# Roots of a row norm laid into memory word by word and read back in token order (attention, dense layer and routed experts on one core)

## The chip, the cores and the metric

One core of a Trainium2 chip runs the whole program. The metric is the device time of one execution in microseconds (us). Of the kernel before, three runs are given: 649.17, 650.56 and 652.78 us, median 650.56.

The engines: TensorE (PE; PEld is its weight load), VectorE (DVE), ScalarE (ACT), GpSimd (POOL) and SyncE (SP), which here only issues transfers. ScalarE issues a few transfers too; a `q` behind an engine's name (ACTq, SPq) marks what its sequencer does. Each engine works through its own list of instructions in order and waits for the others by semaphores.

## The reference

Attention with a bucket mask, then a dense gated layer with a norm of its rows, then a layer of eight routed experts:

```python
scores = scale * np.matmul(q, k.transpose(0, 1, 3, 2))
scores = np.where(mask, scores, -1000000000.0)
...
x = np.ascontiguousarray(attn_out.transpose(0, 2, 1, 3)).reshape(B * S, H * D)   # 1536 tokens x 512
rms = np.sqrt(np.mean(x * x, axis=-1, keepdims=True) + 1e-06)
xn = x / rms * rms_g
g = xn @ w_gate
silu = g * (1.0 / (1.0 + np.exp(-g)))
val = xn @ w_val
x = (silu * val @ w_out)                                                          # then the experts
```

The change touches only how `1 / rms` comes to where `x / rms * rms_g` is formed.

## The kernel before

**Stages.** The attention works through 96 units (a head's 128 queries against 768 keys): a score product on TensorE (`qk`, L530 and L532), the row maximum on VectorE (`stats`, L545), the exponential on ScalarE (`expo`, L559), a scaling by the row sum on GpSimd (`scales`, L554), transposes on TensorE (`back`, L568) with copies out of PSUM by ScalarE or VectorE (`emptied`, L572), and the product with v (L589). The order of all of this is written out by hand: the table `PLAN` gives each step a due time in thousandths of a unit, `attention` collects the steps with `at` and issues them sorted by it. Steps of the dense layer that prepare its weights (L238 to L252) and the norm of its first block of tokens are sorted in among them.

The dense layer (`moe1`) takes three blocks of 512 tokens, and in each twelve slices of 128 of the 1536 hidden features, 36 steps in all. A step splits a slice's weights into a high and a low part (`split`, L317 on ScalarE, L318 on VectorE or GpSimd), forms the gate and value products on TensorE (L345 to L347), the activation (L749 to L753), the low half of the hidden values on VectorE (`h_low`, L758), and adds the down product of the step before (L769 to L771; L771 is the matmul that reads what L758 writes). Products are made of three matmuls of high and low parts each. The weights of later slices are converted on the way (`cv` and `rebias`, L244 to L252 on VectorE, L791 on ScalarE).

**The norm** (`xnorm`, one for each block b): x stands as features by tokens, four chunks of 128 features by 512 tokens. `square` and `add` form the sums of squares; `mean` sums them over the partitions by TensorE, so that one row holds the 512 means; `turn` (L287) moves them by four transfers into a tile `r` of 128 partitions by 4 words, so that token t * 128 + p stands at partition p, word t; `root` (L291, L292 on GpSimd) takes the power -0.5 there; `lay` (L295, issued by ScalarE) writes the 512 roots to a line of device memory, the last row of the output, which is overwritten at the end; `spread` (L298, issued by ScalarE for block 0, by SP for the others) reads that line back into all 128 partitions as `rb`; `scale` (L301 on VectorE, one for each of four chunks) forms x * rms_g * root; `high` (L304, ScalarE) and `low` (L307, VectorE for block 0, GpSimd for the others) split the result for the matmuls.

`lay` writes the line so that each partition's four words stand together, 128 runs of 16 bytes: word 4 * p + t of the line is the root of token t * 128 + p. `scale` therefore reads `rb` with a step of four words, through the views that `ch_` and `rearrange("p (q t) -> p t q")` make.

**Order around the change.** Block 0's norm runs in the attention, at the due times of `PLAN["xn"]` (its entries in order: `square`, `add`, `mean`, `turn`, `root`, `lay`, `spread`, `scale`, `high`, `low`). The norms of blocks 1 and 2 run in the dense block before: with o the first step of that norm, `mean` and `turn` are in step o + 5, `root` in o + 6, `lay` in o + 7 in the list `cal` (after the step's gate and value part), `spread` in o + 7 in the list `post` (after the step's down product), the four `scale` with their `high` in o + 8 and o + 9, the `low` one step after each. SP's and ScalarE's lists hold other transfers and work, and what stands behind a waiting entry waits too.

Of the kernel before, what the change touches and what calls it, by code (L numbers as in the profile page):

```python
# [13 lines left out]
ALU = mybir.AluOpType  # L14
AX = mybir.AxisListType
P = 128
# [29 lines left out]
    "cv": (-4, 4300, 7612, 8983, 10967),  # L46
    "late": 2000,
    "v": 11280,
    "xn": ((54501, 56400), (57300, 58235, 59400), 60900, 62000, 64000, 65000, 69000, (74588, 92089, 73653, 83058), (86240, 93654, 83020, 84060), (89992, 93958, 86081, 95569)),
    "splits": ((-6894, 1, 0, 0), (-10825, 1, 0, 1), (-4899, 0, 0), (1381, 1, 1, 0), (8244, 1, 1, 1)),  # L50
    "ahead": ((215, 2), (3057, 4), (4742, 6), (17871, 8)),
    "batches": (2, 2, 3, 2, 3, 2, 3, 2, 3, 2),
# [27 lines left out]
def tile_kernel(  # L80
# [17 lines left out]
    nc = tc.nc  # L98
# [12 lines left out]
    TPB = TB // P  # L111
# [7 lines left out]
    STT = nc.vector.scalar_tensor_tensor  # L119
# [12 lines left out]
    def f32(ap):  # L132
        return ap.bitcast(F32)
# [19 lines left out]
    def ch4(ap):  # L153
        return ap.rearrange("p (k n) -> p k n", k=4)

    xyt = [ch4(XY[:, i * 2048 : (i + 1) * 2048]) for i in range(3)]
# [34 lines left out]
    gcol = cp.tile([P, NK], F32, name="gcol")  # L191
# [64 lines left out]
    def xpart(b, lo, k):  # L256
        o = X_AT[b] + lo * 2048 + k * TB
        return rg(o, TB)

    def xnorm(b):  # L260

        xf = ch4(BB[:, 0:2048])
        rb = EX[:, 1536:2048]
        sq = rb[:, 0:P]
        line = out[NT - 1 : NT, :]
        st = {}

        def ch_(ap):
            return ap.rearrange("p (t q) -> p t q", t=TPB)

        def square(hf):
            sl = slice(2 * hf, 2 * hf + 2)
            nc.scalar.activation(out=xf[:, sl], in_=xyt[b][:, sl], func=AF.Square)

        def add(x):
            i, j = ((0, 2), (1, 3), (0, 1))[x]
            TT(out=xf[:, i], in0=xf[:, i], in1=xf[:, j], op=ALU.add)

        def mean(ps):
            for t in range(TPB):  # L280
                mm(ps[32 * t : 32 * t + 32, 0:P], lhsT=ones[:, 0:32], rhs=xf[:, 0, t * P : (t + 1) * P], start=True, stop=True)
            (copyV if b else copyA)(out=sq, in_=ps[:, 0:P])

        def turn():
            r = st["r"] = sp.tile([P, 2 * TPB], F32, tag="r", name="r", bufs=2)
            for t in range(TPB):
                dma(out=r[:, t : t + 1], in_=sq[32 * t : 32 * t + 1, :])  # L287

        def root():
            r = st["r"]  # L290
            PTS(r[:, 0:TPB], r[:, 0:TPB], 1.0 / DM, 1e-6, ALU.mult, ALU.add)  # L291
            PTT(out=r[:, TPB:], in0=r[:, 0:TPB], in1=half, op=ALU.pow)  # L292

        def lay():
            nc.scalar.dma_start(out=line.rearrange("o (p t) -> p (o t)", p=P), in_=st["r"][:, TPB:])  # L295

        def spread():
            (dma if b else nc.scalar.dma_start)(out=rb, in_=line.broadcast_to([P, TB]))  # L298

        def scale(k):  # L300
            STT(out=ch_(xf[:, k]), in0=ch_(xyt[b][:, k]), scalar=gcol[:, k : k + 1], in1=rb.rearrange("p (q t) -> p t q", t=TPB), op0=ALU.mult, op1=ALU.mult)  # L301

        def high(k):
            copyA(out=xpart(b, 0, k), in_=xf[:, k])  # L304

        def low(k):
            (PTT if b else TT)(out=xpart(b, 1, k), in0=xf[:, k], in1=f32(xpart(b, 0, k)), op=ALU.subtract)  # L307

        return dict(square=square, add=add, mean=mean, turn=turn, root=root, lay=lay, spread=spread, scale=scale, high=high, low=low)


# [39 lines left out]
    cal = []  # L351
# [327 lines left out]
    def attention():  # L679
# [33 lines left out]
        for x in range(12, 15):  # L713
            at(1000 * (NU - 9) + 500, cv_load, x)
        xn = xnorm(0)
        sq, ad, me, tu, ro, ly, sd, sc, hi_, lo_ = PLAN["xn"]
        for x in range(2):
# [20 lines left out]
    def moe1(rt):  # L738
        total = NBLK * NF
        hs, acc = {}, {}  # L740
        cal = defaultdict(list)
        win = defaultdict(list)
        post = defaultdict(list)
# [52 lines left out]
        for b in range(1, NBLK):  # L796
            xn = xnorm(b)
            o = (b - 1) * NF + (0 if b == 1 else 1)
            for x in range(2):
                cal[o + x].append(lambda f=xn["square"], x=x: f(x))  # L800
            for x in range(3):
                cal[o + 2 + x].append(lambda f=xn["add"], x=x: f(x))
            win[o + 5].append(xn["mean"])
            cal[o + 5].append(xn["turn"])
            cal[o + 6].append(xn["root"])
            cal[o + 7].append(xn["lay"])
            post[o + 7].append(xn["spread"])
            for k in range(NK):
                cal[o + 8 + k // 2].append(lambda xn=xn, k=k: (xn["scale"](k), xn["high"](k)))
                cal[o + 9 + k // 2].append(lambda f=xn["low"], k=k: f(k))  # L810
# [540 lines left out]
    with tc.manual_schedule():  # L1351
        rt = routing()
        attention()
        moe1(rt)
        moe2(rt)
# [92 lines left out]
```

## Time and profile before

| what | value |
|---|---|
| median of three runs | 650.56 us (649.17 to 652.78) |
| the profiled execution's own time | 648.81 us |
| its span, first to last instruction | 646.9 us |
| TensorE busy | 633.8 us, 98% |
| VectorE busy | 533.7 us, 83% |
| ScalarE busy | 399.9 us, 62% |
| GpSimd busy | 268.2 us, 41% |
| granted TensorE clock | 0.998 of full |
| queue of ScalarE's transfers | 720 packets, 0.37 MB |

How to read it: the busy shares are means over stages with different limits. The profiled execution is one execution; its time is its span and some 2 us around it. In a table of waits, each row says which engine waited for which, how long in total, how many times, and the longest. In a timeline each row is one instruction or a run of equal ones: start, busy time, engine, line of the kernel, operation, output and inputs, and in brackets the engine's idle time just before it and what ended it.

### The profile page before, as it was taken

What the parts mean: (1) busy time and instruction counts of PE and PEld (TensorE: products, weight loads), DVE (VectorE), ACT (ScalarE), POOL (GpSimd) and SP (SyncE); (2) the same over time, 40 slices, a digit from 0 to 9 for tenths busy, and PEclk for the clock granted to TensorE, in tenths of its full rate; (3) what the DMA queues carried; (4) which work ended last, traced back from release to release, by engine and by line L of the source; (5) the groups of instructions that cost most, each with busy time, mean ns of one, the idle gap of its engine ahead of it and who ended that gap; (6) DMA issues with size and microseconds to landing.
All of it is one profiled execution on the core that took longest, in us unless ns stands there. A gap on an engine that the chain in (4) does not pass through costs nothing. (4 is left out here: it accounts for less than half of the span.)

```text
span 646.9 us, 10512 instructions
## 1 busy us (share of the span) xinstructions
PE 633.8 (98%) x3598; PEld 504.0 (78%) x3599; DVE 533.7 (83%) x906; ACT 399.9 (62%) x724; POOL 268.2 (41%) x299
## 2 busy tenths in 40 slices
PE   8999999999999999999899999999999999999996
PEld 6777777777777778888788888888888888888884
DVE  6888888898978839998966787899999476999994
ACT  6787888988789746555444333344334353888782
POOL 4677576676756703551622212341124325111211
PEclk9999999999999999999999999999999999999999
DMA  8726538356252215552301000003304015999930
GB/s 250 189 65 193 148 103 218 104 166 151 83 125 103 66 33 183 180 166 74 140 20 53 1 2 0 17 1 128 137 24 173 0 71 175 387 390 389 389 130 26
DMA packets 45991, 84.96 MB, mean 131 GB/s; under 512 B 5708, under 2 KB 19228, under 8 KB 45808
## 3 DMA queue, kind: packets, MB, share of 16 engines
q1 hardware_dynamic: 43856, 80.70, 38.8%
q0 software_dynamic: 1360, 3.20, 1.4%
q8 instruction: 29, 0.48, 0.3%
q10 hardware_dynamic: 720, 0.37, 0.2%
q14 instruction: 26, 0.21, 0.1%
HBM read 67.95 MB, written 5.25 MB: 113 GB/s over the span
## 5 line engine op out<-in xcount | busy, mean ns | idle before, releaser
L318 POOL TENSOR_TENSOR RG<-WW,RG 128x512 fp32r<-128x512 f32 x35 | 68.7, 1962 | 190.1 <-ACT RG L317 182.4
L345 PE MATMUL PS<-RG 128*128 128x512 f32 x288 | 112.5, 391 | 0.0
L346 PE MATMUL PS<-RG 128*128 128x512 f32 x288 | 112.1, 389 | 0.0
L347 PE MATMUL PS<-RG 128*128 128x512 f32 x288 | 112.1, 389 | 0.0
L545 DVE TENSOR_REDUCE peak<-PS 128x1 f32<-128x768 f32 x96 | 91.5, 953 | 20.7 <-PE PS L532 16.0
L559 ACT ACTIVATE WW<-PS,shape 128x768 f32<-128x768 f32 x96 | 95.5, 1000 | 10.9 <-DVE shape L546 9.7
L753 ACT CAST RG<-BB 128x512 fp32r<-128x512 f32 x36 | 22.4, 622 | 109.9 <-DVE BB L751 109.9
L554 POOL TENSOR_SCALAR WW<-WW,rsum 128x768 f32<-128x768 f32 x96 | 87.8, 926 | 4.8
L568 PE MATMUL PS<-cst,WW 128*128 128x128 f32 x576 | 81.4, 277 | 1.0 <-POOL WW L554 0.8
L568 PEld LDWEIGHTS PS<-cst,WW 128*128 128x128 f32 x576 | 64.1, 140 | 20.9 <-POOL WW L554 9.5
L1121 DVE TENSOR_TENSOR RG<-WW,RG 128x1024 fp32r<-128x1024 f32 x64 | 75.2, 1218 | 4.5 <-ACT RG L1119 2.4
L318 DVE TENSOR_TENSOR RG<-WW,RG 128x512 fp32r<-128x512 f32 x73 | 61.4, 879 | 8.3 <-ACT RG L317 8.3
L317 ACT CAST RG<-WW 128x512 fp32r<-128x512 f32 x108 | 61.4, 618 | 7.7 <-PE PS L771 5.0
L1119 ACT CAST RG<-WW 128x1024 fp32r<-128x1024 f32 x64 | 63.9, 1053 | 1.1 <-PE PS L1176 0.8
L345 PEld LDWEIGHTS PS<-RG 128*128 128x128 f32 x288 | 54.1, 188 | 11.8 <-issue 0.8
L347 PEld LDWEIGHTS PS<-RG 128*128 128x128 f32 x288 | 54.1, 188 | 11.3
L346 PEld LDWEIGHTS PS<-RG 128*128 128x128 f32 x288 | 54.1, 188 | 11.1
L771 PE MATMUL PS<-RG 128*128 128x512 f32 x144 | 56.3, 391 | 1.7 <-DVE RG L758 1.7
L769 PE MATMUL PS<-RG 128*128 128x512 f32 x144 | 56.4, 392 | 0.0
L770 PE MATMUL PS<-RG 128*128 128x512 f32 x144 | 56.1, 389 | 0.0
L530 PE MATMUL PS<-RG 128*128 128x512 f32 x192 | 55.5, 369 | 0.2 <-ACT WW L559 0.2
L909 DVE CUSTOM_DVE_ANT_0 EX<-XY,SS 128x512 f32<-128x512 f32 x64 | 50.1, 782 | 1.6
(202 smaller groups left out, 1238.8 us busy)
## 6 DMA issues: line engine op xcount, KB each, us to landing
WW<-in_w SPq DMA_DIRECT2D x32, 1024.0 KB
RG<-RG SPq DMA_DIRECT2D x28, 384.0 KB
WW<-in_kq SPq DMA_DIRECT2D x7, 768.0 KB
SS<-in_wo SPq DMA_DIRECT2D x9, 512.0 KB
SS<-in_wg SPq DMA_DIRECT2D x8, 512.0 KB
SS<-in_wv SPq DMA_DIRECT2D x8, 512.0 KB
WW<-in_v SPq DMA_DIRECT2D x8, 384.0 KB
XY<-in_wg SPq DMA_DIRECT2D x4, 512.0 KB
```

The costliest lines, as they stand in the source:

```text
L317: copyA(out=hi, in_=src)
L318: sub(out=lo, in0=src, in1=f32(hi), op=ALU.subtract)
L345: mm(o, lhsT=h[:, k], rhs=xpart(b, 0, k), start=(k == 0), stop=False)
L346: mm(o, lhsT=h[:, k], rhs=xpart(b, 1, k), start=False, stop=False)
L347: mm(o, lhsT=l[:, k], rhs=xpart(b, 0, k), start=False, stop=(k == NK - 1))
L545: red(out=a[:, 1:2], in_=u_st[u][:, 0:S], axis=AX.X, op=ALU.max, negate=True)
L554: PTS(e_t(x), e_t(x), rsum[:, x % NS : x % NS + 1], 1.0, ALU.mult, ALU.mult)
L559: nc.scalar.activation(out=e_t(u), in_=s[:, 0:S], func=AF.Exp, bias=c, scale=b, accum_out=sums[:, u % NS : u % NS + 1])
L568: nc.tensor.transpose(ps[:, x * P : (x + 1) * P], e_t(u)[:, kt * P : (kt + 1) * P], ident)
L769: mm(acc[t], lhsT=hh[:, sl], rhs=oh, start=(f == 0), stop=False)
L1119: copyA(out=hi[:, sl], in_=src[:, sl])
L1121: f(out=lo[:, sl], in0=src[:, sl], in1=f32(hi[:, sl]), op=ALU.subtract)
```

## The change

Three edits. The line of roots is written so that word t * 128 + p is the root of token t * 128 + p: every one of the 512 words goes to a place of its own (step of 128 words in the line for the words of a partition). `scale` reads `rb`, and x, and writes its output, without the reordering views; the helper `ch_` goes. And the places in the order: in the dense blocks `lay` moves from step o + 7 to the end of step o + 6 (list `post`), and in the attention, in the table, `root` is due at 63700 (64000 before), `lay` at 64500 (65000) and `spread` at 71000 (69000).

```diff
-... 60900, 62000, 64000, 65000, 69000, ...
+... 60900, 62000, 63700, 64500, 71000, ...
...
-        def ch_(ap):
-            return ap.rearrange("p (t q) -> p t q", t=TPB)
-
...
         def lay():
-            nc.scalar.dma_start(out=line.rearrange("o (p t) -> p (o t)", p=P), in_=st["r"][:, TPB:])
+            nc.scalar.dma_start(out=line.rearrange("o (t p) -> p (o t)", p=P), in_=st["r"][:, TPB:])
...
         def scale(k):
-            STT(out=ch_(xf[:, k]), in0=ch_(xyt[b][:, k]), scalar=gcol[:, k : k + 1], in1=rb.rearrange("p (q t) -> p t q", t=TPB), op0=ALU.mult, op1=ALU.mult)
+            STT(out=xf[:, k], in0=xyt[b][:, k], scalar=gcol[:, k : k + 1], in1=rb, op0=ALU.mult, op1=ALU.mult)
...
-            cal[o + 7].append(xn["lay"])
+            post[o + 6].append(xn["lay"])
```

The lists of TensorE, VectorE, GpSimd and SP keep their order; only ScalarE's changes, in three places. (Behind the removed helper the changed file is three lines shorter, so L295 is L292 there, L298 is L295, L317 is L314, L572 is L569 and so on.)

ScalarE in the dense layer, the step in which block 1's norm lays its line (L791 is a weight conversion, L317 the weights' high parts, L749 and L753 the activation). Before:

```order
L791 ACTIVATE BB<-WW 128x512
L791 ACTIVATE SS<-SS 128x512
L317 CAST RG<-WW 128x512 x3
L749 ACTIVATE BB<-PS 128x512
L753 CAST RG<-BB 128x512
L295 DMA out<-r 128x4
```

Of the change:

```order
L788 ACTIVATE BB<-WW 128x512
L788 ACTIVATE SS<-SS 128x512
L292 DMA out<-r 128x4x1
L314 CAST RG<-WW 128x512 x3
L746 ACTIVATE BB<-PS 128x512
L750 CAST RG<-BB 128x512
```

The write has moved ahead of the step's three casts and its activation; in block 2 it moves in the same way.

ScalarE in the attention, where block 0's line is laid and read (L572 copies transposes out of PSUM, L559 is the exponential, L599 the copy of the product with v). Before:

```order
L599 COPY XY<-PS 128x256
L572 COPY BB<-PS 128x3x128
L295 DMA out<-r 128x4
L572 COPY BB<-PS 128x3x128
L559 ACTIVATE WW,sums<-PS,shape 128x768 x2
L572 COPY EX<-PS 128x3x128 x2
L572 COPY BB<-PS 128x3x128 x2
L559 ACTIVATE WW,sums<-PS,shape 128x768 x2
L572 COPY WW<-PS 128x3x128
L599 COPY XY<-PS 128x256
L572 COPY WW<-PS 128x3x128
L298 DMA EX<-out 128x512
```

Of the change:

```order
L292 DMA out<-r 128x4x1
L569 COPY BB<-PS 128x3x128 x2
L556 ACTIVATE WW,sums<-PS,shape 128x768 x2
L569 COPY EX<-PS 128x3x128 x2
L569 COPY BB<-PS 128x3x128 x2
L556 ACTIVATE WW,sums<-PS,shape 128x768 x2
L569 COPY WW<-PS 128x3x128
L596 COPY XY<-PS 128x256
L569 COPY WW<-PS 128x3x128 x2
L556 ACTIVATE WW,sums<-PS,shape 128x768 x2
L569 COPY WW<-PS 128x3x128
L295 DMA EX<-out 128x512
```

The write has moved ahead of one copy, and the read behind one copy, two exponentials and another copy.

## Rows read from the trace of the kernel before

**Rows 1.** The page: busy time and share of the span of each engine.

```profile
PE 633.8 (98%) x3598; PEld 504.0 (78%) x3599; DVE 533.7 (83%) x906; ACT 399.9 (62%) x724; POOL 268.2 (41%) x299
```

**Rows 2.** Waits of TensorE, whole span: waited for: us in total, times, longest.

```profile
PE PS L771 <- DVE RG L758: 1.7, 1, 1.7
```

**Rows 3.** Timeline of TensorE, dense block 1: start us, us busy, [idle before].

```profile
316.44 0.39 PE L770 MATMUL PS<-RG 128*128 128x512 f32 x1
318.49 0.50 PE L771 MATMUL PS<-RG 128*128 128x512 f32 x1 [1.66 <-DVE RG L758]
```

**Rows 4.** Timeline of VectorE, the same stretch and the step before.

```profile
300.70 2.19 DVE L301 SCALAR_TENSOR_TENSOR BB<-XY,gcol,EX 128x512 f32<-128x512 f32 x2
...
303.83 1.28 DVE L248 SCALAR_TENSOR_TENSOR WW<-SS,WW 128x512 int32<-128x512 int32 x2
...
310.64 4.12 DVE L301 SCALAR_TENSOR_TENSOR BB<-XY,gcol,EX 128x512 f32<-128x512 f32 x2
...
317.75 0.68 DVE L758 TENSOR_TENSOR RG<-BB,RG 128x512 fp32r<-128x512 f32 x1
```

**Rows 5.** Timeline of GpSimd, the same stretch.

```profile
310.45 3.38 POOL L307 TENSOR_TENSOR RG<-BB,RG 128x512 fp32r<-128x512 f32 x2
```

**Rows 6.** Single lines of VectorE: duration ns least/median/most, first and last start, shape.

```profile
L301 DVE SCALAR_TENSOR_TENSOR BB<-XY,gcol,EX x12: 1134/1150/2161, 173.2 to 419.9; 128x512 f32<-128x512 f32 x12
L486 DVE SCALAR_TENSOR_TENSOR RG<-WW,kqs,RG x14: 1007/1010/1354, 16.9 to 182.9; 128x768 fp32r<-128x768 f32 x14
```

**Rows 7.** Timelines of VectorE, ScalarE and TensorE, attention, 173 to 181 us.

```profile
173.16 1.18 DVE L301 SCALAR_TENSOR_TENSOR BB<-XY,gcol,EX 128x512 f32<-128x512 f32 x1
174.82 1.16 DVE L301 SCALAR_TENSOR_TENSOR BB<-XY,gcol,EX 128x512 f32<-128x512 f32 x1
176.51 0.94 DVE L545 TENSOR_REDUCE peak<-PS 128x1 f32<-128x768 f32 x1
177.82 0.99 ACT L559 ACTIVATE WW<-PS,shape 128x768 f32<-128x768 f32 x1 [0.90 <-DVE shape L546]
173.75 0.88 PE L568 MATMUL PS<-cst,WW 128*128 128x128 f32 x6
174.38 0.59 PE L530 MATMUL PS<-RG 128*128 128x512 f32 x2
178.06 0.88 PE L568 MATMUL PS<-cst,WW 128*128 128x128 f32 x6
178.95 0.61 PE L530 MATMUL PS<-RG 128*128 128x512 f32 x2
179.76 0.49 PE L568 MATMUL PS<-cst,WW 128*128 128x128 f32 x3
180.44 0.55 PE L568 MATMUL PS<-cst,WW 128*128 128x128 f32 x3 [0.19 <-ACT WW L572]
```

**Rows 8.** Timelines of ScalarE, SP and GpSimd around write and read; one line's issues.

```profile
153.40 0.35 ACTq L295 DMA_DIRECT2D out<-r  x1
167.04 0.86 ACT L572 COPY WW<-PS 128x384 f32<-128x384 f32 x2 [1.19 <-PE PS L568]
283.24 1.02 POOL L292 TENSOR_TENSOR r<-r,half 128x4 f32<-128x4 f32 x1
285.61 0.67 ACT L791 ACTIVATE SS<-SS 128x512 f32<-128x512 f32 x1
289.28 0.60 ACT L749 ACTIVATE BB<-PS 128x512 f32<-128x512 f32 x1 [1.45 <-PE PS L347]
295.15 0.34 SPq L298 DMA_DIRECT2D EX<-out  x1
401.36 0.34 ACTq L295 DMA_DIRECT2D out<-r  x1
402.90 0.34 SPq L298 DMA_DIRECT2D EX<-out  x1
L287 SPq DMA_DIRECT2D r<-EX x12: 476/599/602, 145.3 to 386.4; - x12
```

More of the change, by code (lines that the diff above doesn't have):

```diff
@@ L48 @@
     "v": 11280,
-    "xn": ((54501, 56400), (57300, 58235, 59400), 60900, 62000, 64000, 65000, 69000, (74588, 92089, 73653, 83058), (86240, 93654, 83020, 84060), (89992, 93958, 86081, 95569)),
+    "xn": ((54501, 56400), (57300, 58235, 59400), 60900, 62000, 63700, 64500, 71000, (74588, 92089, 73653, 83058), (86240, 93654, 83020, 84060), (89992, 93958, 86081, 95569)),
     "splits": ((-6894, 1, 0, 0), (-10825, 1, 0, 1), (-4899, 0, 0), (1381, 1, 1, 0), (8244, 1, 1, 1)),
```

## The prediction

> **What bounds the kernel now.** I read the page first, then the table of waits of TensorE, then the timelines of the engines around the three places where the norm runs (one in the attention, one in each of the first two dense blocks). The page says TensorE is busy 98% of the span, VectorE 83% [rows 1]. The reader should take from it that a VectorE saving is worth something only where TensorE stands still for VectorE. The waits name one such place: a matmul of the down product (L771) waits 1.7 us for VectorE's L758, once [rows 2]. That is the largest wait of TensorE in the whole run. In TensorE's timeline L770 starts at 316.44, L771 at 318.49, where matmuls of this shape otherwise follow each other every 0.23 us [rows 3]: 318.49 - 316.44 - 0.23 = **1.82 us lost**.
>
> Why is L758 late? It subtracts to make the low half of the hidden values. On VectorE it stands behind the norm's scaling (L301), which this change edits. In the dense step before, two L301 took 2.19 us; in this step two took 4.12 us, and from 310.64 until L758 starts at 317.75 no row of VectorE has idle time ahead of it; the first and the last of that chain stand in [rows 4]. The longer pair falls together with two of GpSimd's own subtractions, L307, from 310.45 to 313.83 [rows 5]. So the lost 1.82 us are the end of a chain that is all VectorE, and whatever shortens L301 there arrives at TensorE undiminished, until the 1.82 us are used up.
>
> **The change part by part.** *The scaling reads in order.* L301 runs 12 times, at 1.13 to 2.16 us, median 1.15 [rows 6]. Before, its second input is read at a step of 4 words; afterwards all operands lie in order. How long is the same operation in order? Two L248, also scalar_tensor_tensor over 128x512 with two inputs in SBUF, take 1.28 us where two L301 take 2.19 [rows 4]: (2.19 - 1.28) / 2 = 0.46 us each. L248 has an immediate for its scalar, so I looked for one with a column as L301 has it: L486, 768 columns in 1.01 us [rows 6], that is 0.67 us for 512 in proportion. Both agree, so I take **0.46 us saved per L301**. L248 reads at a step of two words and is not slow; so a step alone costs nothing, and the step of four is the remaining difference. Bounds: 0 if something else makes L301 slow, 0.46 if the step does.
>
> The Trainium skill (SBUF — State Buffer, Door 1: The DMA port swizzle) says SBUF is read in lines of 16 bytes, that each access on a new line pays, and in the same note that fp32 may stride up to 4 for free. The step here is just 4; by the last half of that sentence L301 would save nothing and the sum below would be zero, by the first half it saves as I have it.
>
> *Dense block 1.* Two pairs of L301 lie ahead of the late L758: the pair at 300.70 and that at 310.64 [rows 4]. VectorE has no idle time to name between them, and the casts of ScalarE and the subtractions of GpSimd in this stretch come after VectorE's results, so the first pair's 2 x 0.46 moves the second pair forward. The second pair stands in turn with GpSimd's L307, but what it needs for itself still shrinks by 0.46 each. Together 4 x 0.46 = 1.84 us, against 1.82 lost: the wait disappears, nearly to the digit. At the low end only the first pair counts (0.92), because GpSimd's subtractions would hold the second as before. I take **1.82**, since both pairs lie on the same unbroken chain.
>
> *Attention.* Here TensorE's wait is small but has the same cause. Two L301 at 173.16 and 174.82 push the row maximum L545 to 176.51; ScalarE's exponential waits 0.90 us for VectorE and starts at 177.82 [rows 7]. Some four us earlier on TensorE six transposes from 173.75 are followed by a score product at 174.38, 0.63 later or 0.105 for each; from 178.06 the same takes until 178.95, 0.89 later: 0.26 lost. Three transposes begun at 179.76 are followed by three more only at 180.44, 0.68 later where 0.33 would do: 0.35 lost, because ScalarE's copies come after the late exponentials [rows 7]. Two L301 give back 0.92 in this chain, more than 0.26 and 0.35 need: **0.61**, at least 0. The other two L301 of the attention and the four of dense block 2 save 6 x 0.46 on VectorE, where TensorE shows no wait (the one in [rows 2] is the only one on VectorE above 0.2 us); that cover is TensorE's own work, and I price them at 0.
>
> *The line is written word by word.* 128 runs of 16 bytes become 512 of 4. In dense block 2 the write is issued at 401.36 and the read that waits for it at 402.90 [rows 8]: at most 1.54 us to land. No row shows 512 words. Lower bound 1.54; upper bound, if four times the pieces take four times as long, 6.2 (an estimate from that row). I take about 2.5, nearer the low row, since 1.54 also holds what each transfer costs once. Neither end matters. In block 1 the write now stands right behind the activation of 285.61 to 286.28, and the read is not issued before 295.15 [rows 8]: 8.9 us. The read itself had landed before L301 of 300.70, so 5.55 us are enough for it. In the attention the write moves one copy ahead of its place at 153.40, and the read to just ahead of the copies of 167.04, into 1.19 us in which ScalarE waits for TensorE [rows 8]: over 12 us for the write, and 5 or more for the read until L301 at 173.16. The Trainium skill (DMA: Bandwidth & Descriptors, Rules for kernel authors) says a strided last dimension becomes one descriptor per element and should be made contiguous instead: a rule against this edit. By that rule the write grows to 512 descriptors, which the sum as it stands has room for; how long one of them takes no run here shows yet.
>
> *Issuing it.* The write's issue took 0.34 us; transfers of 128 single words (L287) take 0.60 [rows 8]. Between 0.34 and, for 4 x 128 words, 2.4 us (an estimate) on ScalarE's queue. In block 1 the casts behind it wait; after them ScalarE is idle 1.45 us until 289.28 [rows 8], so that much is free. In the attention nothing covers it: up to 2.06 us in one place. I take 0.34, the same instruction's own row.
>
> *The write a step ahead.* It may now wait for the root. In block 1 GpSimd starts the root at 283.24 and ends it 1.02 us later, at 284.26; ScalarE comes to the write at 286.28 [rows 8]. No wait, so nothing behind it on ScalarE's queue is held; block 2 has the same order of steps. SP's queue, which issues the read in both blocks, keeps its order.
>
> **Sum.** -1.82 - 0.61 = -2.43 us. The profiled execution took 648.81 us (span 646.9), so 646.4. It lies 1.75 us under the median of the runs, 650.56; on the median, **648.1 us**, 0.37% less. What a measurement of this kernel can tell from no change is about 0.5%, 3.25 us: I forecast a real gain that mostly will not be told from none.
>
> **The rivals.**
> 1. *L301 is no faster.* Its time would come from something other than the step (three operands and a column scalar, say). For it: no row shows L301 itself in order. Against: L486 has these operands and runs at full pace [rows 6]. Gain 0, 650.5 us. Chance 0.10. The half sentence of the Trainium skill on strides that are free comes to this rival.
> 2. *Half the chain.* GpSimd's subtractions hold the second pair as before, or another wait comes first: 0.92 instead of 1.82 in block 1, and 0 to 0.61 in the attention. For it: 4.12 against 2.19 us [rows 4, 5] shows a partner that sets the pace. 649.0 to 649.6 us. Chance 0.18.
> 3. *The words are slow: slower.* One mechanism: the 512 single words land so late that the read, and behind it L301 with all of VectorE's queue, has to wait. It decides above 8.9 us of landing in block 1. At 16 us, VectorE would stand 7 us longer there, about as long in block 2, and ScalarE's queue 2 us in the attention, 13 to 16 us on no gain: 663 to 667 us. Against: 6.2 us is the most that the row of 1.54 gives. Chance 0.05.
> 4. *The issue is dear.* Up to 2.06 us on ScalarE's queue in the attention, if its copies and exponentials are then late for TensorE: takes back most of the gain, 648.5 to 650.2 us. For it: the single words of L287 cost 0.60 where the present write costs 0.34 [rows 8]. Against: both move 128 pieces, so the difference isn't their number. Chance 0.07.
>
> My forecast has the remaining 0.60.
>
> **How the numbers follow.** Range: the forecast reaches from 646.2 (with 1.9 us for the scatter of a median, whose runs lay between 649.17 and 652.78) to 650; rivals 1, 2 and 4 reach up to 650.6. So 646.2 to 650.7; rival 3 and some scatter stay outside. Faster by over 0.5% needs 3.25 us, more than both waits that I found; only scatter of 0.8 us or more on top of the forecast brings it: a quarter of 0.60, 0.15. Slower by over 0.5%: rival 3, and a little scatter on rivals 1 and 4, 0.06. The rest is the same: 0.79.
>
> **What would show it.** Right: L301 at about 0.68 us; the wait of L771 for L758 in the dense step near 316 gone or under 0.2 us; L758 starting 1.8 us earlier against the matmuls; the attention's transposes near 180 without the 0.35. The queue of the write has 384 packets more for each line laid, with nothing waiting for them. Wrong: L301 still near 1.1 us (rival 1); L771 still waiting about 0.9 (rival 2); L301 or ScalarE waiting for a DMA on the line (rival 3); ScalarE's queue held for a microsecond or more at the write (rival 4).

## The result, and the profile after

The changed kernel is slower. Its median is 658.44 us (655.61 to 660.68, six runs), beside 649.88 us for the kernel before (648.95 to 652.78, six runs): ratio 1.0119, interval 1.0093 to 1.0145 (the two medians alone stand as 1.013). The forecast was 648.1 us, range 646.2 to 650.7. The profiled execution took 660.68 us, span 658.9 us.

The page, to be set beside [rows 1]; the second row is the queue of ScalarE's transfers (packets, MB, share), which had 720 packets before:

```profile
PE 642.1 (97%) x3599; PEld 508.3 (77%) x3599; DVE 528.4 (80%) x906; ACT 400.7 (61%) x724; POOL 267.3 (41%) x299
...
q10 hardware_dynamic: 1872, 0.37, 0.3%
```

VectorE works 5.3 us less, as meant, and yet the span is 12.0 us longer. The queue has 1152 packets more for the same bytes: 3 x 384, as foretold. Line numbers are three lower than before.

The edited operation did get faster. One line of VectorE, to be set beside L301 of [rows 6]:

```profile
L298 DVE SCALAR_TENSOR_TENSOR BB<-XY,gcol,EX x12: 742/746/1779, 183.5 to 430.6; 128x512 f32<-128x512 f32 x12
```

That is 1.150 to 0.746 us, 0.40 each where I had 0.46. The waits of TensorE over the whole span, to be set beside [rows 2]:

```profile
PE PS L768 <- DVE RG L755: 2.5, 2, 1.4
PE PS L527 <- DMA RG<-RG: 2.4, 1, 2.4
PE PS L529 <- DMA RG<-RG: 1.8, 1, 1.8
```

The wait that was to vanish is there twice (L768 is L771 of before), and two waits for transfers are new; none of these transfers belongs to the norm. The same four waits in TensorE's timeline:

```profile
176.07 0.58 PE L527 MATMUL PS<-RG 128*128 128x512 f32 x2 [2.38 <-DMA RG<-RG]
178.41 0.98 PE L529 MATMUL PS<-RG 76*128 76x512 f32 x2 [1.75 <-DMA RG<-RG]
...
320.72 0.50 PE L768 MATMUL PS<-RG 128*128 128x512 f32 x1 [1.38 <-DVE RG L755]
...
330.26 0.50 PE L768 MATMUL PS<-RG 128*128 128x512 f32 x1 [1.09 <-DVE RG L755]
```

**Where the 12 us lie.** I set the start of each matmul against the start of the same matmul before and followed the difference through the span.
- The first 18 us: +4.0 us. The first matmuls of this execution ran at a lower pace (three that start at 8.00, 8.35 and 8.71 us before start at 10.26, 10.90 and 11.54). This start differs from one execution to the next: 0.1 to 2.4 us in experiments 1 to 4 and 6 to 8, and 4.1 and 4.2 in 5 and 9, whose extra writes start only after 350 us. So it isn't the change's. Without it 8.0 us remain, near the 8.6 by which the medians differ.
- The attention between 169 and 173 us on the scale of before: +7.2 us; then -0.26 at 178.95 and -0.35 at 180.44, the two gains that I had forecast there, in full.
- Dense block 1: +1.5 where L768 waits anew, -0.57 at the place of the old wait.
- Dense block 2: no loss.

**The attention.** A table of stretches (us, busy time of each engine with its instructions, granted clock of TensorE, DMA share, GB/s moved). First the kernel before, from 2.6 us behind the issue of its write at 153.40:

```profile
156.00:162.00 6.00, 6.00 (x48) 4.90 (x47) 5.00 (x9) 5.07 (x12) 3.51 (x6) 1.00 1.01 278
162.00:169.00 7.00, 7.00 (x54) 5.01 (x53) 5.99 (x11) 5.36 (x12) 5.35 (x8) 1.00 0.55 176
```

The kernel after; its write is issued at 156.43:

```profile
162.00:169.00 7.00, 7.00 (x57) 5.11 (x55) 5.75 (x12) 6.05 (x13) 4.57 (x7) 1.00 0.76 39
169.00:175.00 6.00, 4.69 (x34) 3.21 (x32) 4.36 (x8) 3.20 (x8) 3.12 (x4) 1.00 1.01 236
175.00:182.00 7.00, 4.18 (x18) 3.29 (x22) 1.18 (x2) 3.30 (x8) 3.33 (x5) 0.67 0.45 148
```

In the first of these stretches, from 5.6 to 12.6 us behind the write's issue, the DMA engines are busy for a share of 0.76 and move 39 GB/s. In the kernel before they move 278 GB/s at 1.01 and 176 at 0.55, and at the same distance from its write (159.03 to 166.03) 220 at 0.87. So each byte holds them five to six times longer. Then the delayed bytes come at once (236). TensorE is short of work in the second and third stretch, and behind its two waits its granted clock falls: 0.67 in the third stretch, that is, part of it at 1.2 GHz instead of 2.4 (from 177.42 to 184.25, 0.50). 4.13 of the 7.2 us are the two waits above, most of the rest is matmuls at the lower clock behind them. Who was held up is seen in the queues. ScalarE's timeline, SP's timeline, and SP's table of waits (155 to 185 us), each from the kernel after:

```profile
156.43 0.41 ACTq L292 DMA_DIRECT2D out<-r  x1
...
172.15 0.36 ACTq L295 DMA_DIRECT2D EX<-out  x1
172.61 0.86 ACT L569 COPY WW<-PS 128x384 f32<-128x384 f32 x2 [2.80 <-DMA WW<-in_kq]
```

```profile
156.76 3.37 SPq L392 DMA_DIRECT2D WW<-in_kq  x1
```

```profile
SPq L511 <- DMA RG<-RG: 7.3, 1, 7.3
SPq L490 <- DMA RG<-RG: 4.1, 1, 4.1
```

The load of the next keys and queries (768 KB), issued 0.33 us behind the write, held SP for 3.37 us where the same issue took 1.16 before. SP then waits 7.3 us for the transfers that put rows in place for the next score products, and TensorE waits for those. ScalarE's queue stands 2.80 us for the load as well: what stands there is the line's own read (L295), which is not issued before 172.15, when the load has landed. What that hold costs by itself was not tried; both of TensorE's waits end with transfers of SP, and SP had waited for other transfers, not for ScalarE.

**Dense block 1.** The same table of stretches. Before, while the three weight loads issued from 286.14 move:

```profile
287.00:296.00 9.00, 9.00 (x41) 7.48 (x40) 8.55 (x16) 4.77 (x10) 4.13 (x1) 1.00 0.64 184
```

After, while the same three loads, issued from 296.81, should move:

```profile
297.00:306.00 9.00, 9.00 (x41) 7.48 (x40) 8.55 (x16) 3.30 (x6) 4.13 (x1) 1.00 0.15 22
306.00:312.00 6.00, 6.00 (x28) 4.96 (x27) 1.87 (x4) 2.76 (x5) 0.00 (x0) 1.00 0.99 352
```

22 GB/s while the words are landing, where the same loads moved at 184 before; then 352. The timelines of ScalarE, SP and VectorE of the kernel after show whom that hits:

```profile
295.26 0.38 ACTq L292 DMA_DIRECT2D out<-r  x1
295.69 0.68 ACT L788 ACTIVATE BB<-WW 128x512 f32<-128x512 f32 x1
...
308.40 0.67 ACT L788 ACTIVATE EX<-SS 128x512 f32<-128x512 f32 x1 [3.88 <-DMA SS<-in_wo]
```

```profile
296.81 0.34 SPq L238 DMA_DIRECT2D SS<-in_wo  x1
...
305.68 0.65 SPq L295 DMA_DIRECT2D EX<-out  x1
```

```profile
311.10 1.29 DVE L315 TENSOR_TENSOR RG<-WW,RG 128x512 fp32r<-128x512 f32 x2 [4.13 <-ACT RG L314]
...
314.04 1.41 DVE L298 SCALAR_TENSOR_TENSOR BB<-XY,gcol,EX 128x512 f32<-128x512 f32 x2
...
323.18 3.35 DVE L298 SCALAR_TENSOR_TENSOR BB<-XY,gcol,EX 128x512 f32<-128x512 f32 x2
```

A weight load issued 1.55 us behind the write lets ScalarE begin only at 308.40, 11.6 us later. ScalarE stands 3.88 us for it, VectorE behind ScalarE 4.13 us, and TensorE behind VectorE 1.38. The line's own read (305.68), and L298, wait for nothing here. But it was close. By the trace's updates of its semaphore the write landed at 304.54, 9.3 us behind its issue, which is more than the 8.9 us of room that the prediction gave it. It had 10.42 us, because ScalarE's queue issued it at 295.26, ahead of the run of the two L788 (295.69 and 296.27) that stand before it in the list.

**Block 2** gives the landing itself, since there the read waits for the write. ScalarE's and SP's rows, to be set beside the pair 401.36 and 402.90 of [rows 8], and the wait:

```profile
404.98 0.38 ACTq L292 DMA_DIRECT2D out<-r  x1
```

```profile
413.16 0.34 SPq L295 DMA_DIRECT2D EX<-out  x1
```

```profile
SPq L295 <- DMA out<-r: 12.9, 1, 12.9
```

**8.2 us from issue to landing, where it was 1.54.** The DMA engines have sent the 512 packets by 406.27 us, 1.3 us after the issue; the other seven pass, without a packet on any queue, before the write is reported as done. No load is under way in this block that anything waits for, so nothing is lost here. In the attention, among the loads, the same write took 10.7 us by its semaphore's updates.

### The profile page after: what moved, and what is told of

Its sections match the earlier page's. It is cut to its first block, busy times and chain, and to the rows that moved or that the text cites. A ratio compares the mean times of both kernels' runs of the same rounds, so it can differ in the third digit from the quotient of the medians.

```text
span 658.9 us, 10515 instructions
## 1 busy us (share of the span) xinstructions
PE 642.1 (97%) x3599; PEld 508.3 (77%) x3599; DVE 528.4 (80%) x906; ACT 400.7 (61%) x724; POOL 267.3 (41%) x299
## 5 line engine op out<-in xcount | busy, mean ns | idle before, releaser
L551 POOL TENSOR_SCALAR WW<-WW,rsum 128x768 f32<-128x768 f32 x96 | 86.3, 911 | 4.8
L314 ACT CAST RG<-WW 128x512 fp32r<-128x512 f32 x108 | 61.4, 619 | 7.3 <-PE PS L768 4.6
L768 PE MATMUL PS<-RG 128*128 128x512 f32 x144 | 56.4, 392 | 2.5 <-DVE RG L755 2.5
L529 PE MATMUL PS<-RG 76*128 76x512 f32 x192 | 51.1, 348 | 1.8 <-DMA RG<-RG 1.8
```

The lines of the kernel that those rows point to most:

```text
L314: copyA(out=hi, in_=src)
L551: PTS(e_t(x), e_t(x), rsum[:, x % NS : x % NS + 1], 1.0, ALU.mult, ALU.mult)
```

## Experiments

My theory behind these profiles: the loss is the 512 separate words, and it falls on other transfers. Rivals: the new places in the order do it (a write early enough to meet the loads of the next step); the line's reader pays after all; or any transfer of that many pieces costs this much. The runs of one group shared their runs of the kernel before.

**1. The new places without the words.** The changed kernel with runs of 16 bytes and the read at a step of four again:

```diff
-            nc.scalar.dma_start(out=line.rearrange("o (t p) -> p (o t)", p=P), in_=st["r"][:, TPB:])
+            nc.scalar.dma_start(out=line.rearrange("o (p t) -> p (o t)", p=P), in_=st["r"][:, TPB:])
...
-            STT(out=xf[:, k], in0=xyt[b][:, k], scalar=gcol[:, k : k + 1], in1=rb, op0=ALU.mult, op1=ALU.mult)
+            STT(out=ch_(xf[:, k]), in0=ch_(xyt[b][:, k]), scalar=gcol[:, k : k + 1], in1=rb.rearrange("p (q t) -> p t q", t=TPB), op0=ALU.mult, op1=ALU.mult)
```

> The changed kernel with the line written in runs of 16 bytes again and read with a step of four words; the new places of write and read stay. Theory W (512 single words hold up the device memory for some 7 us, and with it every other transfer): the loss is gone, 649 to 651 us, L301 back at 1.13 us or more, the wait of L771 for L758 back at 1.7 us. Rival Q (the new places are at fault: the read of the attention, issued later, draws another semaphore and waits for a load that is still under way): the loss stays, 655 to 658 us, with ScalarE waiting about 2.5 us at the attention's read.

650.49 us beside 650.12; ratio 1.0007 (0.9987 to 1.0028). The waits of TensorE and the line of VectorE are those of before:

```profile
PE PS L771 <- DVE RG L758: 1.6, 1, 1.6
```

```profile
L301 DVE SCALAR_TENSOR_TENSOR BB<-XY,gcol,EX x12: 1132/1158/2173, 174.9 to 421.7; 128x512 f32<-128x512 f32 x12
```

The places cost nothing and bring nothing. The loss belongs to the words, or to the reading in order, which went back with them; experiments 3 and 4 exclude the second.

**2. The words in the old places.** The kernel before with the write and the read of the change:

```diff
-            nc.scalar.dma_start(out=line.rearrange("o (p t) -> p (o t)", p=P), in_=st["r"][:, TPB:])
+            nc.scalar.dma_start(out=line.rearrange("o (t p) -> p (o t)", p=P), in_=st["r"][:, TPB:])
...
-            STT(out=ch_(xf[:, k]), in0=ch_(xyt[b][:, k]), scalar=gcol[:, k : k + 1], in1=rb.rearrange("p (q t) -> p t q", t=TPB), op0=ALU.mult, op1=ALU.mult)
+            STT(out=xf[:, k], in0=xyt[b][:, k], scalar=gcol[:, k : k + 1], in1=rb, op0=ALU.mult, op1=ALU.mult)
```

> The kernel before with the line written word by word and read in order, all places as before. Theory W: as slow as the changed kernel or slower, 655 to 660 us, since the write has less time ahead of its reader in the dense blocks (1.5 to 2.5 us before, 8 needed, so VectorE's queue would wait 5 us or so for it in each). Rival Q: 647 to 649 us, the gain of the scaling alone.

661.47 us, ratio 1.0163 (1.0136 to 1.0191): 3 us worse than the change by the medians, and above the 655 to 660 that I expected. The write of block 1 is issued at 300.83 and its read at 310.35, 9.5 us later. TensorE's waits, and VectorE's:

```profile
PE PS L771 <- DVE RG L758: 6.1, 3, 4.1
PE PS L530 <- DMA RG<-RG: 2.0, 1, 2.0
PE PS L532 <- DMA RG<-RG: 1.8, 1, 1.8
```

```profile
DVE BB L301 <- DMA EX<-out: 10.6, 2, 5.3
```

Here the line's reader does pay: L301 waits 10.6 us in the two blocks together, which is what the change's step ahead avoids. In the attention the loss is there as in the change (two waits for RG<-RG, +6.5 us by starts of matmuls).

**3. Token order by other means, old places.** The reader can have the words in order and the write can keep its 16 bytes, if the transfers of `turn` already lay four neighbouring tokens into each partition:

```diff
-                dma(out=r[:, t : t + 1], in_=sq[32 * t : 32 * t + 1, :])
+                dma(out=r[32 * t : 32 * t + 32, 0:TPB], in_=sq[32 * t : 32 * t + 1, :])
...
-            STT(out=ch_(xf[:, k]), in0=ch_(xyt[b][:, k]), scalar=gcol[:, k : k + 1], in1=rb.rearrange("p (q t) -> p t q", t=TPB), op0=ALU.mult, op1=ALU.mult)
+            STT(out=xf[:, k], in0=xyt[b][:, k], scalar=gcol[:, k : k + 1], in1=rb, op0=ALU.mult, op1=ALU.mult)
```

> The kernel before, but the turn puts four neighbouring tokens into each partition (32 runs of 16 bytes per transfer instead of 128 words), so that runs of 16 bytes lay the line in token order already; the scaling reads in order; all places as before. Measures what reading in order is worth with no word written. Theory W and rival Q both: 2.0 to 2.4 us under the kernel before, 647 to 648.5 us, L301 at 0.75 us, the wait of L771 for L758 under 0.3 us. If the scaling gains nothing: 650 us.

648.26 us beside 650.12; ratio 0.998 (0.996 to 0.9999). The line of VectorE, and the place of [rows 3] in TensorE's timeline:

```profile
L301 DVE SCALAR_TENSOR_TENSOR BB<-XY,gcol,EX x12: 742/746/1778, 175.2 to 418.5; 128x512 f32<-128x512 f32 x12
```

```profile
317.72 0.39 PE L770 MATMUL PS<-RG 128*128 128x512 f32 x1
318.20 0.50 PE L771 MATMUL PS<-RG 128*128 128x512 f32 x1
```

The wait of L771 is all but gone: it starts 0.48 us behind L770 instead of 2.05, so 1.57 of the 1.82 us come back and 0.25 stay. In the attention 0.26 us come back at 178.95 and 0.35 at 180.44, by starts of the same matmuls. These are the two terms of my sum, 1.82 and 0.61.

**4. The same in the new places.** Experiment 3 with `root`, `lay` and `spread` where the change has them:

```diff
-... 60900, 62000, 64000, 65000, 69000, ...
+... 60900, 62000, 63700, 64500, 71000, ...
...
-            cal[o + 7].append(xn["lay"])
+            post[o + 6].append(xn["lay"])
```

> As e3_turn_in_runs, with the write and read at the new places of the changed kernel. Theory W: as e3, 647 to 648.5 us. Rival Q: 653 to 656 us, the loss of the places without the words.

648.48 us, ratio 0.9979 (0.996 to 0.9997); 0.61 and 1.55 us at the same places. It equals experiment 3: with a write that lands at once the places don't matter. Both are 0.2% faster than the kernel before; the intervals only just exclude no difference, and the starts of the matmuls carry the reading.

**5. Landing, measured by itself.** Six writes from the same engine into rows of the output that are filled later, in a stretch with few other transfers, each followed on SP by a read of one of its words, so that the read's issue marks the landing:

```diff
...
+            (14, free(1503).rearrange("(p t) -> p t", p=P), TPB),
+            (15, free(1500).rearrange("(t p) -> p t", p=P), TPB),
+            (16, free(1400, 16).rearrange("(t p x) -> p t x", p=P, x=16)[:, :, 0], TPB),
+            (17, out[1000:1512, 0:1].rearrange("(t p) o -> p (t o)", p=P), TPB),
+            (21, free(1501)[0:P].rearrange("(p t) -> p t", p=P), 1),
+            (22, free(1502).rearrange("(p x) -> p x", p=P)[:, 0:1], 1),
...
+            post[n].append(lambda dst=dst, w=w: nc.scalar.dma_start(out=dst, in_=half[:, 0:w]))
+            post[n].append(lambda dst=dst, y=y: dma(out=junk[0:1, y : y + 1], in_=dst[0:1, 0:1]))
```

> The kernel before with six extra writes of constants from ScalarE in quiet steps of the second dense block, each followed by a read of one word on SP's queue that waits for its landing; nobody uses them. In order: 128 runs of 16 bytes; 512 words side by side; 512 words 64 bytes apart; 512 words 2048 bytes apart; 128 words side by side; 128 words 16 bytes apart. The time from the write's issue to the read's issue is the landing. Theory W1 (what costs is that many single writes fall into the same small stretch of memory, one after the other): about 1.5, 8, 2 to 3, 2 to 3, 2 to 3.5, 2 to 3 us. Rival W2 (each single write costs the same wherever it goes, some 13 ns): about 1.5, 8, 8, 8, 3, 3 us. Rival W3 (bytes and pieces don't matter, the 8 us came from other traffic): 1.5 us for all. The kernel's time stays within 2 us of before.

The second, third and fourth write in ScalarE's timeline, and their reads in SP's:

```profile
363.94 0.39 ACTq L845 DMA_DIRECT2D out<-half  x1
...
372.10 0.38 ACTq L845 DMA_DIRECT2D out<-half  x1
...
380.49 0.38 ACTq L845 DMA_DIRECT2D out<-half  x1
```

```profile
373.24 0.23 SPq L846 DMA_DIRECT2D junk<-out  x1
...
374.81 0.22 SPq L846 DMA_DIRECT2D junk<-out  x1
...
382.36 0.22 SPq L846 DMA_DIRECT2D junk<-out  x1
```

512 words side by side: 9.3 us. The same 512 words 64 bytes apart: 2.7 (at most: they were issued 1.14 us before the 512 ahead of them had landed); 2048 bytes apart: 1.9. So it isn't the number of pieces, it is how close together they land, and rivals W2 and W3 fall. 128 words: 7.4 side by side, 1.4 at 16 bytes apart. Theory W1, right in kind, had 2 to 3.5 for the 7.4. The kernel took 653.72 us in its one run, 3.4 over the kernel before where I had allowed 2; its first 18 us, ahead of the first extra write, are 4.1 us longer than in the profiled execution of the kernel before.

**6. More words that nobody reads.** The kernel before, and in the attention a second write of the 512 roots, word by word, into another row of the output, right behind the line's own:

```diff
+            if b == 0:
+                nc.scalar.dma_start(out=out[NT - 2 : NT - 1, :].rearrange("o (t p) -> p (o t)", p=P), in_=st["r"][:, TPB:])
```

> The kernel before with one more write in the attention: the same 512 roots word by word into a row that nobody reads, right behind the line's own write in runs of 16 bytes. Doubles the suspected cost alone; order, line, read and scaling as before. Theory W: the transfers under way stand still for some 7 us though nothing waits for the row itself: 653 to 657 us, TensorE waiting for transfers of rows into RG near 165 to 175 us. Rival (only whoever waits for the words is held): 650 to 651 us.

653.82 us beside 650.29; ratio 1.0045 (1.0012 to 1.0079). TensorE has a new wait (L534 is L532 of before):

```profile
PE PS L534 <- DMA RG<-RG: 1.1, 1, 1.1
```

A write without a reader slows the kernel, through the same row transfers. That shows that the price falls on others. It is smaller than in the change (+1.6 us in the profiled execution by starts of matmuls, against 7.2); this write was issued at 154.14, 0.51 us behind the keys' load, the change's 0.33 us ahead of it. The order of the two alone does not explain it: in experiment 2 the write goes out 0.09 us behind the load (155.73 and 155.64), and the two waits are there in full. Why the loss is so much smaller here stays open.

**7. Words in the attention alone.** The changed kernel with runs of 16 bytes and the read at a step of four in blocks 1 and 2:

```diff
-            nc.scalar.dma_start(out=line.rearrange("o (t p) -> p (o t)", p=P), in_=st["r"][:, TPB:])
+            at_ = "o (p t) -> p (o t)" if b else "o (t p) -> p (o t)"
+            nc.scalar.dma_start(out=line.rearrange(at_, p=P), in_=st["r"][:, TPB:])
...
```

> The changed kernel with words and reading in order for the first block's norm alone; in the dense blocks runs of 16 bytes and a read with a step of four words, at the new places. Theory W by the trace of the changed kernel: the attention keeps its 7 us of loss, the dense block loses nothing more but keeps its wait of 1.8 us: 655 to 658 us. If the dense blocks carried the loss: 649 to 651 us.

656.6 us beside 650.29; ratio 1.0096 (1.0059 to 1.0132). TensorE's waits:

```profile
PE PS L529 <- DMA RG<-RG: 3.3, 1, 3.3
PE PS L770 <- DVE RG L757: 1.6, 1, 1.6
PE PS L531 <- DMA RG<-RG: 1.5, 1, 1.5
```

The two attention waits are there in full and block 1 is as before the change. One write of 2 KB carries most of the loss: 6.3 us by the medians.

**8 and 9. How few words, and does their order count?** The frame of experiment 5 with other writes. In 8: fewer words, and pieces of 8 bytes. In 9: neighbouring words written by other partitions than neighbouring ones. Three of the twelve writes, the first two from 8 and the third from 9:

```diff
...
+            (16, free(1501)[0:16].rearrange("(p x) -> p x", x=1), half[0:16, 0:1]),
+            (17, free(1502)[0:64].rearrange("(p x) -> p x", x=1), half[0:64, 0:1]),
...
+            (14, free(1503)[0:64].rearrange("(a b) -> b a", a=4), half[0:64, 0:1]),
...
```

> The kernel before with six other extra writes in the same quiet steps, each followed by a read of one word that waits for its landing. In order: 128 words 8 bytes apart; 256 runs of 8 bytes side by side; 16 words side by side; 64 words side by side; 4 words side by side; 128 runs of 8 bytes side by side. Known from the probes before: 128 runs of 16 bytes side by side 1.4 us, 128 words 16 bytes apart 1.4 us, 128 words side by side 7.4 us, 512 side by side 9.3 us. Theory L (separate writes into one 64-byte line go one after the other, some 0.4 us each, and lines go side by side; four in a line still hide): 16 words side by side 7 us, 64 words 7 us, 4 words 1.5 to 2 us, 8 bytes apart or runs of 8 bytes (8 in a line) 3 to 4.5 us. Rival M (the number of side-by-side words in all counts): 16 words 2 us, 64 words 4 us, 256 runs of 8 bytes 8 us. Rival N (what counts is whether a write fills 16 bytes' own place, so any two in the same 16 bytes wait): all six 5 us or more.

> The kernel before with six extra writes in the quiet steps, as in the two runs of probes. In order: 64 words that fill the same 256 bytes, but neighbouring partitions 64 bytes apart, so that the partitions next to each other don't write neighbouring words; 128 words in the same way (512 bytes, neighbouring partitions 64 bytes apart); 32 words side by side; 64 words side by side (again); 128 words side by side (again); 128 words that fill the same 512 bytes with neighbouring partitions 128 bytes apart, so that every fourth partition writes the neighbouring word. Theory E (a transfer works through neighbouring partitions one behind the other, and a word that goes next to the one just written waits for it): 1.4, 1.4, about 3, 6.7, 7.4, about 3 us. Theory L (only how many words fall into one line of memory counts, whoever writes them): 6.7, 7.4, 1.4 to 7, 6.7, 7.4, 7.4 us.

From the issue of the write to that of its read, in us, all probes of 5, 8 and 9, by how many separate pieces fall into 256 neighbouring bytes:

| pieces in 256 bytes | writes | us |
|---|---|---|
| 1 and 4 | 512 words, 2048 and 64 bytes apart | 1.9, 2.7 |
| 4 | 4 words in all | 1.2 |
| 16 | 16 words; 128 words 16 bytes apart; 128 runs of 16 bytes | 1.3; 1.4; 1.4 |
| 32 | 32 words; 128 words 8 bytes apart; 128 and 256 runs of 8 bytes | 3.2; 2.8; 3.0, 3.5 |
| 64 | 64 words (three writes) and 128 words (four) | 6.5 to 7.0; 6.7 to 7.4 |
| 64 | 512 words | 9.3 |

My picture before 8, a price for pieces within 64 bytes, fell with the 16 words: 1.3 us where it wanted 7. Rival M fell with the 64 words (6.7 where it wanted 4), rival N with the 4 and the 16 words, which took less than 5. The picture before 9, that neighbouring words collide because neighbouring partitions write them at the same moment, fell too: 6.5 us with neighbours dealt out, 7.0 without. What fits the 18 probes (but for the 2.7 us, which the write ahead may have lengthened) is a price for each further piece within a stretch of some 256 bytes: from 16 to 64 words 5.1 to 5.7 us more, about 0.1 us a word. Stretches side by side are worked through mostly at the same time (128 words cost hardly more than 64). Why memory does that, and whether 256 is the exact size, these runs don't show.

## Why the prediction was wrong

**The failed step is "upper bound, if four times the pieces take four times as long, 6.2 ... Neither end matters."** Two things in it failed, and by them the sum held no term for the write at all; the runs showed +7.2 us in the attention and +1.5 in block 1.

- *The bound.* The words took 8.2 us in block 2, 9.3 in block 1, 10.7 in the attention, and 9.3 with little else moving (experiment 5). I scaled by the number of pieces, and the number isn't what counts: 512 of them landed in 1.9 to 2.7 us when far apart. The nearest row was of runs of 16 bytes, 16 to a stretch of 256 bytes, and up to there a landing stays at 1.2 to 1.4 us; the price begins between 16 and 32. A straight line from that row could not show it.
- *"Neither end matters".* I asked only who waits for the line. Rival 3 had the right sign and the wrong victim: it let the line's reader and L301 wait, and decided above 8.9 us in block 1. In the change neither waits there, though the landing took 9.3 us: the write had 10.42, since it was issued earlier than I had worked out. The price falls on whatever is moving in the meantime: 39 GB/s instead of 220 in the attention, 22 instead of 184 in block 1. Experiment 6 shows it without any reader, and experiment 7 that the attention alone carries most of it. Rival 3's own mechanism is real, but in the old places: experiment 2 has its waits of L301, 10.6 us in two.

**The gain was right in mechanism and a little too large.** L301 shortens by 0.40 us instead of 0.46, and rival 1 (no faster) falls. Scaling L486 in proportion was at fault: 1.010 us for 768 columns and 0.746 for 512 differ by 0.26, so some 0.2 us of either does not go with the columns (an estimate from these two rows). The terms 1.82 and 0.61 measured 1.57 and 0.61 in experiment 3, 1.55 and 0.61 in experiment 4; so rival 2 (half the chain) falls as well. The partner that it feared is there: the pair beside GpSimd's subtractions still takes 3.35 us, where the other pair takes 1.41. But it does not hold the gain back, for 3.35 is 0.77 less than in [rows 4]. The forecast of 648.1 us is close to what the same gain gives without the words, 648.3 to 648.5; in part by luck, since it started from a median of 650.56 and those runs from 650.12. In the change itself only 0.57 of the 1.57 shows, because VectorE had to catch up 4.13 us of waiting on the same chain.

**Issuing.** 0.38 to 0.41 us against 0.34: rival 4 falls. Another queue's issue, SP's load of the keys, took 3.37 us instead of 1.16; that is not the cause of the loss, for in experiments 2 and 7, which lose 6.5 and 8.3 us at the same place of the attention, it took 1.16 and 1.77.

**One descriptor per element.** The Trainium skill (DMA: Bandwidth & Descriptors, Rules for kernel authors) spoke against one descriptor per element, and I gave it a sentence and no chance. The trace agrees with the descriptors (384 packets more for each line) and with the direction, but not on the count as the reason: 512 descriptors far apart cost 0.5 to 1.3 us more than 128 runs of 16 bytes (1.4). The same page of the Trainium skill (Specifications) says that below 512 bytes the DMA reads, modifies and writes. The runs of 16 bytes lie below that too, and land in 1.4 us; so that line alone gives no price.

## What to carry to other kernels

Don't lay many separate small pieces into the same few hundred bytes of device memory: change the layout one step earlier, on chip, so that the write goes out in runs (here 16 bytes were enough). Price a slow transfer by what else is moving while it lands, not only by who reads it; an engine-side gain of some 2 us was outweighed by one 2 KB write whose landing nobody was waiting for. And bound an unseen transfer by its shape (size of a piece and distance between pieces), not only by its number of pieces.

## What the hardware showed that I had not expected

- 64 single words written into 256 neighbouring bytes take 6.5 to 7.0 us to land, 16 words 1.3; 512 words 2048 bytes apart take 1.9.
- Meanwhile other loads crawl: 22 GB/s for nine microseconds where the same loads moved at 184 before, then 352.
- The write's issue did not wait for the run of the instructions ahead of it on ScalarE's queue: it went out at 295.26, the two L788 ahead of it in the list ran from 295.69 and 296.27.
- An input read at a step of exactly four words makes the 128x512 operation take 1.15 us instead of 0.746 (a step of two words, in L248, 0.68); the Trainium skill (SBUF — State Buffer, Door 1) counts a step of up to 4 fp32 as free, and here the measurement decides: not of 4.
